# Another order for the last pairs of a windowed attention: blocks turned and low parts subtracted on other engines

## The chip, the cores and the metric

The kernel runs on one core of one Trainium2 chip, as one program. The metric is the device time of one execution, in microseconds (us). The core has five engines that each work through their own queue in order: PE (matrix products), DVE and ACT (elementwise work), POOL (elementwise work) and SP, which issues the transfers between the chip's main memory and the on-chip memory (SBUF). Products land in PSUM, a small memory of banks. Engines wait for each other by semaphores only.

## What is computed

Attention with a window and a few global keys, and behind it a "soft" mixture of experts on its output. The attention has 4 batches, 8 heads, 768 positions and a head size of 64:

```python
scores = scale * np.matmul(q, k.transpose(0, 1, 3, 2))
is_global = pos[None, :] < int(n_global)               # 8
is_local = (rel >= 0) & (rel < int(n_local))           # 96
bias = -slopes[:, None, None] * dist[None, :, :]
scores = np.where(is_global | is_local, scores + bias, -1000000000.0)
a = softmax(scores)                                     # over the keys
x = np.matmul(a, v)                                     # as 3072 tokens x 512
logits = x @ phi                                        # 32 slots, 4 of each of 8 experts
d, c = softmax(logits, over tokens), softmax(logits, over slots)
slot_out[e] = np.maximum((d.T @ x)[e] @ w1[e], 0) @ w2[e]
y = c @ slot_out
```

## The kernel before

**Pairs.** The attention goes through 16 pairs of heads, numbered 0 to 15 (four pairs of each batch; pairs 11 and 15 end the third and the fourth batch). Each pair is worked through in steps, and a step is one small function with one or a few instructions of one engine. The last number in a step's name is the head of the pair (0 or 1), or a part of a tile.

- `load_qk`, `load_v` (SP): the pair's inputs. `raw` tiles hold queries and keys, in turn for even and odd pairs.
- `scores u k` (PE, k = 0, 1, 2): products of keys and queries for a third of the blocks, into one of two PSUM tiles `sc`, in turn.
- `biased u k` (DVE): adds the table of distances, writes to a tile `tb` (three of them, in turn), and keeps a running maximum. The same `sc` tile is free for the next scores after it.
- `max_t` (PE) and `max_r` (DVE): the maximum over the partitions.
- `exponential u i` (ACT): in place on `tb`, for head i.
- `w_hi u i` (ACT): the weights rounded to 16 bits, into `ph`. `w_lo u i part` (POOL) or `w_lo_dve` (DVE): what the rounding lost, for a third of the blocks; three parts make the low half.
- `v_hi` (POOL), `v_hi_act` (ACT) or `v_hi_dve` (DVE), and `v_lo` (DVE): the same split for the values.
- `values u i` (PE): 39 products of the halves, into a bank `x`. It needs all three low parts; the next `w_hi` of the same head overwrites what it reads.
- `ev_sums`, `ev_recs`, `ev_mul u i` (DVE): the division, into token rows `xn`. They free the bank `x`.
- `tr u k` (PE): turns blocks of `xn`. `tr_copy u k` (ACT) or `tr_copy_dve u k` (DVE) copies the turned block out of PSUM into a tile `xt` (there are three, in `xta`, `xtt` and `tt`).
- `logits u` (PE) for odd pairs, then `logits_half` (ACT) or `logits_all` (DVE); and at the end of each batch `strip_max` (DVE), `strip_exp` (ACT), `by_token` (PE), `by_token_copy` and `lnat_copy` (ACT), `dispatch` (PE) and `dispatch_sum` (DVE), which bring the slots' inputs up to date.

**PSUM banks.** `max_t`, `tr`, `logits`, `by_token` and `dispatch` share two banks "m" in turn. Each of these steps can start only when the result of the step two before it (among these) has been read out.

**Order.** There is no scheduler: the list `ORDER` (line 55) has 607 steps, and each engine gets its instructions in the order in which the steps stand there. Two steps of one engine never pass each other.

**Weights.** Some 32 MB of expert weights stream in all the while. Ten tiles are theirs from the start. The steps `free n` (SP) load more of them into tiles of the attention, each when its last reader is done; the order of the last `free` of each tile also decides which piece of the weights it holds.

**Behind the list** come the last softmax over the slots, the hidden layer, the output products and the output's transfers (`last_dispatch` and the list `TAIL`). Three filler products (line 556) of `warm_x` stand at the very front of it.

Of the kernel before, what the change touches and what calls it, by code (L numbers as in the profile page):

```python
# [28 lines left out]
QW = KB + WIN  # L29
# [278 lines left out]
def tile_attention_moe(ctx: ExitStack, tc: tile.TileContext, qk, v, phi, w1, w2, nn, out):  # L308
    nc = tc.nc
# [58 lines left out]
    phi_ = [t[:, 0:PH].bitcast(F16) for t in pht]  # L368
# [84 lines left out]
    def blocks(w):  # L453
        return w[:, 0:6 * PB].rearrange("p (s c) -> p s c", c=PB)
# [44 lines left out]
    def tb(u):  # L499
        return tbuf[u % 3]  # L500
# [99 lines left out]

    def w_hi_dve(u, i):
        nc.vector.tensor_copy(out=blocks(phi_[i])[:, :, 0:QW], in_=tb(u)[:, i].rearrange("p (s c) -> p s c", c=QW))

    def w_lo(u, i, part, engine=None):
        c = slice(2 * part, 2 * part + 2)
        (engine or nc.gpsimd).tensor_tensor(out=blocks(plo_[i])[:, c, 0:QW], in0=tb(u)[:, i].rearrange("p (s c) -> p s c", c=QW)[:, c],  # L606
                                            in1=blocks(phi_[i])[:, c, 0:QW], op=ALU.subtract)

    def w_lo_dve(u, i, part):
        w_lo(u, i, part, nc.vector)  # L610

    def values(u, i):
        ph, pl = phi_[i], plo_[i]
        vh, vl = vhi[u % 2], vlo[u % 2]
        x = sums(u, i)
        ops = []
        for t in range(NJ):
            for j, c in ((t, PCOL[t]), (t - 1, PCOL[t - 1] + KB)):
                if j >= 0:
                    for w, vv, d in ((ph, vh, D + 1), (ph, vl, D), (pl, vh, D + 1)):  # L620
                        ops.append((t, c, w, vv, j, d))
        for z, (t, c, w, vv, j, d) in enumerate(ops):
            nc.tensor.matmul(out=x[:, (D + 1) * t:(D + 1) * t + d], lhsT=w[:, c:c + P], rhs=vv[:, j, i, 0:d],  # L623
                             start=(z == 0), stop=(z == len(ops) - 1), skip_group_check=True)
# [253 lines left out]

    def table_rest_act(u):
        table.rest(nc.scalar.copy)  # L880

    def table_pair_act(p):
        table.pair_act(p)

    def table_pair(p):
        table.pair(p)

    steps = dict(piece=piece_of, free=free, extra=extra, load_phis=load_phis, bcast=bcast, keys=keys, table_rest=table_rest, table_rest_act=table_rest_act, table_pair_act=table_pair_act, warm_x=warm_x, warm=warm,
                 table_even=table_even, table_odd=table_odd, table_pair=table_pair, load_qk=load_qk, load_v=load_v, v_hi=v_hi, v_hi_act=v_hi_act, v_hi_dve=v_hi_dve, v_lo=v_lo,
                 scores=scores, biased=biased, max_t=max_t, max_r=max_r, exponential=exponential, w_hi=w_hi, w_lo=w_lo, w_lo_dve=w_lo_dve, w_hi_dve=w_hi_dve,  # L890
                 values=values, ev_sum=ev_sum, ev_rec=ev_rec, ev_sums=ev_sums, ev_recs=ev_recs, ev_mul=ev_mul, tr=tr, tr_copy=tr_copy, tr_copy_dve=tr_copy_dve,
                 logits=logits, logits2=logits2, logits_half=logits_half, logits_all=logits_all, strip_max=strip_max, strip_exp=strip_exp,
                 strip_sum=strip_sum, by_token=by_token, by_token_copy=by_token_copy, lnat_copy=lnat_copy, dispatch=dispatch, dispatch_sum=dispatch_sum)
    late_constants()
    for name, u, *args in ORDER:
        steps[name](u, *args)
    left = LeftBanks()
    put_rest = last_dispatch(left, lambda: warm_x(last))
    att.close()


    tail = ExitStack()
# [327 lines left out]
```

## Time and profile before

| | us |
|---|---|
| median of 3 runs | 185.19 (184.1 to 185.4) |
| the profiled execution, its own time | 184.54 |
| its span, first to last instruction | 182.5 |
| PE at work | 170.5 (93% of the span) |
| DVE at work | 141.6 (78%) |
| ACT at work | 125.8 (69%) |
| POOL at work | 97.2 (53%) |

The span is what the trace covers; times in the trace count from its start. In the trace one instruction, or a few alike, is one row. An engine's "idle before" is the time that it stood before an instruction, with the work that ended the wait. The end of a product on PE is modelled, so a row may reach a little into the next one. All engines but SP are busy for most of the first 120 us, which are the attention; after that mainly PE and the transfers are.

### The profile page before, as it was taken

What the parts mean: (1) busy time and instruction counts of PE and PEld (TensorE: products, weight loads), DVE (VectorE), ACT (ScalarE), POOL (GpSimd) and SP (SyncE); (2) the same over time, 40 slices, a digit from 0 to 9 for tenths busy, and PEclk for the clock granted to TensorE, in tenths of its full rate; (3) what the DMA queues carried; (4) which work ended last, traced back from release to release, by engine and by line L of the source; (5) the groups of instructions that cost most, each with busy time, mean ns of one, the idle gap of its engine ahead of it and who ended that gap; (6) DMA issues with size and microseconds to landing.
All of it is one profiled execution on the core that took longest, in us unless ns stands there. A gap on an engine that the chain in (4) does not pass through costs nothing.

```text
span 182.5 us, 6745 instructions
## 1 busy us (share of the span) xinstructions
PE 170.5 (93%) x2805; PEld 125.8 (69%) x2805; DVE 141.6 (78%) x378; ACT 125.8 (69%) x164; POOL 97.2 (53%) x129
## 2 busy tenths in 40 slices
PE   8999899999999999999999998999899999999820
PEld 2567689797878877979888986875533256677710
DVE  5999999999998989899999999987867303346430
ACT  3499989999989999988999999953302120345320
POOL 6926689859799498797998996750010000000000
PEclk9999999999999999999999999999999999999975
DMA  6999999958998956789887399999999999989892
GB/s 186 420 399 390 413 400 392 392 192 307 381 391 338 383 156 247 250 310 379 288 344 276 89 310 376 407 370 416 416 387 409 408 404 404 380 303 405 347 334 65
DMA packets 15306, 61.41 MB, mean 337 GB/s; under 512 B 1698, under 2 KB 2850, under 8 KB 13474
## 3 DMA queue, kind: packets, MB, share of 16 engines
q1 hardware_dynamic: 15264, 60.89, 87.8%
q8 instruction: 24, 0.39, 0.9%
q14 instruction: 16, 0.13, 0.2%
q10 hardware_dynamic: 2, 0.00, 0.0%
HBM read 54.59 MB, written 6.29 MB: 334 GB/s over the span
## 4 chain that ended last, share of the span: by engine, by line


## 5 line engine op out<-in xcount | busy, mean ns | idle before, releaser
L606 POOL TENSOR_TENSOR ph<-tb,ph 128x432 f16<-128x432 f32 x83 | 85.9, 1066 | 18.9 <-ACT ph L599 15.8
L596 ACT ACTIVATE tb<-tb,nb 128x1296 f32<-128x1296 f32 x32 | 43.7, 1374 | 0.9 <-DVE nb L592 0.8
L623 PEld LDWEIGHTS <-ph 128*128 128x128 f16 x1248 | 40.7, 97 | 4.2 <-issue 2.8
L599 ACT CAST ph<-tb 128x1296 f16<-128x1296 f32 x32 | 40.6, 1271 | 2.8 <-PE x L623 0.9
L623 PE MATMUL x<-v,ph 128*128 128x65 f16 (+1 forms) x1209 | 42.0, 193 | 0.3 <-POOL ph L606 0.2
L571 PE MATMUL sc<-raw 64*128 64x216 f32 (+1 forms) x392 | 40.8, 340 | 0.0
L571 PEld LDWEIGHTS sc<-raw 64*128 64x128 f32 x392 | 32.3, 186 | 6.0 <-issue 3.5
L651 DVE CUSTOM_DVE_ANT_1 xn<-x,rc 120x448 f32<-120x448 f32 x31 | 18.3, 622 | 2.1 <-PE m L774 1.6
L580 DVE CUSTOM_DVE_ANT_1 tb<-sc,tt,mx 128x864 f32<-128x864 f32 x16 | 17.8, 1115 | 1.1 <-DVE mx L580 0.5
L549 DVE SCALAR_TENSOR_TENSOR v<-vt,v 128x896 f16<-128x896 f32 x14 | 16.2, 1159 | 0.0
L663 PE MATMUL m<-ident,xn 120*128 120x120 f32 x98 | 14.7, 276 | 0.2 <-DVE xmax L651 0.2
L663 PEld LDWEIGHTS m<-ident,xn 120*128 120x128 f32 x98 | 10.0, 141 | 2.7 <-issue 1.5
L104 PE MATMUL hp<-wp,sl 128*32 128x512 f32 x80 | 10.9, 594 | 0.3 <-ACT sl L99 0.3
L606 DVE TENSOR_TENSOR ph<-tb,ph 128x432 f16<-128x432 f32 x13 | 9.6, 765 | 0.0
L580 DVE CUSTOM_DVE_ANT_1 tb<-sc,xtt,mx 128x864 f32<-128x864 f32 x8 | 8.9, 1115 | 0.4 <-DVE mx L580 0.2
L580 DVE CUSTOM_DVE_ANT_1 tb<-sc,xta,mx 128x864 f32<-128x864 f32 x8 | 8.9, 1112 | 0.2
L542 ACT ACTIVATE v<-vt 128x896 f16<-128x896 f32 x9 | 8.6, 951 | 0.0
L205 PE MATMUL cp<-sos,ct 32*128 32x128 f32 (+1 forms) x120 | 8.4, 334 | 0.2 <-ACT ph L218 0.2
L159 PE MATMUL o<-wp,ht 128*32 128x128 f32 x256 | 8.4, 275 | 0.0
L580 DVE CUSTOM_DVE_ANT_1 tb<-sc,tt 128x864 f32<-128x864 f32 x8 | 8.4, 1050 | 0.0
L159 PEld LDWEIGHTS o<-wp,ht 128*32 128x32 f32 x256 | 6.6, 109 | 1.5 <-issue 1.0
L910 POOL MEMSET ht<- 128x536 f32 x1 | 0.5, 544 | 13.1 <-PE ld L848 13.1
(235 smaller groups left out, 283.5 us busy)
## 6 DMA issues: line engine op xcount, KB each, us to landing
raw<-in_qk_dram SPq DMA_DIRECT2D x14, 832.0 KB, 5.7
wp<-in_w_dram SPq DMA_DIRECT2D x10, 1024.0 KB, 8.0
wp<-in_w_dram SPq DMA_DIRECT2D x15, 512.0 KB, 9.0
vt<-in_v_dram SPq DMA_DIRECT2D x14, 448.0 KB, 5.5
tb<-in_w_dram SPq DMA_DIRECT2D x3, 1024.0 KB, 8.1
wp<-in_qk_dram SPq DMA_DIRECT2D x2, 832.0 KB, 9.5
raw<-in_w_dram SPq DMA_DIRECT2D x2, 832.0 KB, 4.5
ph<-in_w_dram SPq DMA_DIRECT2D x2, 768.0 KB, 9.9
```

Of the source, the lines that this page charges most:

```text
L104: self.nc.tensor.matmul(out=hp[n][32 * s:32 * s + 32, :], lhsT=slv(a, c, s), rhs=w1(4 * a + s, c // 2)[:, (c % 2) * DF + 512 * n:(c % 2) * ...
L159: nc.tensor.matmul(out=o[32 * s:32 * s + 32, o0:o0 + w], lhsT=ht[:, k:k + 32], rhs=w2(4 * a + s, half)[:, at:at + w], start=(a == 0 and c ...
L542: nc.scalar.activation(out=vhi[u % 2][:, :, :, 0:D], in_=vraws(u), func=AF.Copy, scale=V_SC)
L549: nc.vector.scalar_tensor_tensor(out=vlo[k].rearrange("p j i d -> p (j i) d"), in0=vraws(u).rearrange("p j i d -> p (j i) d"), scalar=V_SC ...
L571: nc.tensor.matmul(out=z[:, i, at:at + n], lhsT=r_[r, KCOL[j]:KCOL[j] + KR], rhs=r_[r, KW + KB * j:KW + KB * j + n], start=True, stop=True)
L580: nc.vector.tensor_tensor_reduce(out=tb(u)[:, :, BW * k:BW * k + BW], in0=sc[(3 * u + k) % 2][:, :, 0:BW], in1=table.unit(u % NP, k), scal ...
L596: nc.scalar.activation(out=t, in_=t, func=AF.Exp, bias=nbs[u], scale=T_SC)
L599: nc.scalar.copy(out=blocks(phi_[i])[:, :, 0:QW], in_=tb(u)[:, i].rearrange("p (s c) -> p s c", c=QW))
L606: (engine or nc.gpsimd).tensor_tensor(out=blocks(plo_[i])[:, c, 0:QW], in0=tb(u)[:, i].rearrange("p (s c) -> p s c", c=QW)[:, c], in1=bloc ...
L623: nc.tensor.matmul(out=x[:, (D + 1) * t:(D + 1) * t + d], lhsT=w[:, c:c + P], rhs=vv[:, j, i, 0:d], start=(z == 0), stop=(z == len(ops) - ...
L651: nc.vector.tensor_tensor_reduce(out=xnb[(u // 2) % 3][:, :, c:c + D], in0=by_query(u, i)[:, :, 0:D], in1=rcs.pop((u, i)).unsqueeze(2).to_ ...
L663: nc.tensor.transpose(out=m[:, at:at + KB], in_=xnb[(u // 2) % 3][:, t, P * (p % 2):P * (p % 2) + P], identity=ident[0:KB, 0:KB])
```

## The change

Up to `w_hi 11 0` (the high part of pair 11, the 420th step) the list stays as it is. The 187 steps behind it are put in another order. The set of steps is the same but for 16 that are traded between engines:

- turned blocks: 9 1, 11 0 and 12 1 are now copied by DVE, and 9 0, 13 1 and 12 0 by ACT (each was on the other of the two); 11 1 and 15 0 stay on DVE;
- low parts: (13, 0, 0), (14, 0, 0), (15, 1, 0) and (15, 1, 2) go from POOL to DVE, and (12, 0, 2), (14, 0, 2), (15, 0, 1) and (15, 0, 2) from DVE to POOL;
- the values' high half: pair 14 goes from ACT to POOL, pair 15 from POOL to DVE.

The `free` steps are regrouped as well. Before, the last six were v16 and ph0 pieces, `tb0`, and the three `xt` tiles; now `tb0` comes last of all. The diff, cut to its core (the list is one line; of its 187 moved steps the first few are shown):

```diff
@@ -52,7 +52,7 @@
-ORDER = [
...
-('exponential', 11, 0), ('w_hi', 11, 0), ('w_lo', 11, 0, 0), ('max_t', 12), ('max_r', 12), ('dispatch', 7), ('scores', 13, 1), ('w_lo', 11, 0, 1), ('biased', 13, 0),
...
+('exponential', 11, 0), ('w_hi', 11, 0), ('w_lo', 11, 0, 1), ('dispatch', 7), ('biased', 13, 0), ('w_lo', 11, 0, 0), ('ev_recs', 10), ('v_hi_act', 12), ('ev_mul', 10, 0),
...
@@ -597,6 +597,16 @@
+    def w_hi_part(u, i, part, copy=nc.scalar.copy):
+        c = slice(2 * part, 2 * part + 2)
+        copy(out=blocks(phi_[i])[:, c, 0:QW], in_=tb(u)[:, i].rearrange("p (s c) -> p s c", c=QW)[:, c])
+
+    def w_hi_part_dve(u, i, part):
+        w_hi_part(u, i, part, nc.vector.tensor_copy)
+
+    def w_hi_part_pool(u, i, part):
+        w_hi_part(u, i, part, nc.gpsimd.tensor_copy)
```

The new functions are entered in the table of steps, but no step of the list uses them. Lines behind 600 have a number that is higher by 10 in the changed kernel.

The first of three places is DVE's queue from the second `biased` of pair 15 to its third (the two rows each of L580; the maximum of the third is what `max_t 15` turns). Before:

```order
L580 ISA tb_95,mx<-sc_171,xtt,mx 128x2x432
L580 ISA mx 128x1
L672 COPY tt<-m 128x288
L549 SCALAR_TENSOR_TENSOR v_100<-vt,v_100 128x896
L580 ISA tb_95,mx<-sc_172,xtt,mx 128x2x432
```

And in the changed kernel:

```order
L580 ISA tb_95,mx<-sc_171,xtt,mx 128x2x432
L580 ISA mx 128x1
L754 COPY state<-al 128x1
L616 TENSOR_TENSOR ph_98<-tb_96,ph_98 128x2x216
L682 COPY tt<-m 128x480
L549 SCALAR_TENSOR_TENSOR v_100<-vt,v_100 128x896
L682 COPY tt<-m 128x288
L580 ISA tb_95,mx<-sc_172,xtt,mx 128x2x432
```

Between the two stand now, beside `v_lo 14` (L549) and one copy, also `strip_sum 3` (L754), the low part (13, 0, 0) (L616) and a second copy of a turned block of pair 11.

The second place is DVE's queue around `logits_all 11` (L710 before, L720 after) and `strip_max 11` (L727, L737), from the last division of pair 13 (L651, L661) on. Before:

```order
L651 ISA xn_106,xmax<-x,rc 120x7x64
L651 ISA xmax 120x1
L744 COPY state<-al 128x1
L710 ISA lsb,al<-m,lsb 96x240
L710 ISA al 96x1
L710 ISA lsb,al<-m,lsb 32x48
L710 ISA al 32x1
L727 TENSOR_SCALAR state<-al,state 128x1
L672 COPY xtt<-m 128x288
L606 TENSOR_TENSOR ph_98<-tb_97,ph_98 128x2x216 x2
L549 SCALAR_TENSOR_TENSOR v_100<-vt,v_100 128x896
```

And in the changed kernel:

```order
L661 ISA xn_106,xmax<-x,rc 120x7x64
L661 ISA xmax 120x1
L616 TENSOR_TENSOR ph_98<-tb_97,ph_98 128x2x216
L720 ISA lsb,al<-m,lsb 96x240
L720 ISA al 96x1
L720 ISA lsb,al<-m,lsb 32x48
L720 ISA al 32x1
L737 TENSOR_SCALAR state<-al,state 128x1
L616 TENSOR_TENSOR ph_98<-tb_97,ph_98 128x2x216
L545 TENSOR_SCALAR v_100<-vt 128x14x64
L682 COPY xta<-m 128x288
L549 SCALAR_TENSOR_TENSOR v_100<-vt,v_100 128x896
```

One of the two low parts of pair 14 (L606, L616) has moved ahead of `logits_all 11`, and `v_hi_dve 15` (L545) now stands ahead of `v_lo 15` (the last row of each).

The third place is the end of POOL's queue, from the low parts of (13, 0) on; `ph_99` is head 1 and `ph_98` head 0; `tb_96`, `tb_97` and `tb_95` here are pairs 13, 14 and 15. Before:

```order
L606 TENSOR_TENSOR ph_98<-tb_96,ph_98 128x2x216 x3
L539 TENSOR_SCALAR v_100<-vt 128x14x64
L606 TENSOR_TENSOR ph_99<-tb_97,ph_99 128x2x216 x3
L606 TENSOR_TENSOR ph_98<-tb_97,ph_98 128x2x216
L606 TENSOR_TENSOR ph_99<-tb_95,ph_99 128x2x216 x3
```

And in the changed kernel:

```order
L539 TENSOR_SCALAR v_100<-vt 128x14x64
L616 TENSOR_TENSOR ph_98<-tb_96,ph_98 128x2x216 x2
L616 TENSOR_TENSOR ph_99<-tb_97,ph_99 128x2x216 x3
L616 TENSOR_TENSOR ph_98<-tb_97,ph_98 128x2x216
L616 TENSOR_TENSOR ph_99<-tb_95,ph_99 128x2x216
L616 TENSOR_TENSOR ph_98<-tb_95,ph_98 128x2x216 x2
```

Before, POOL ended with the three low parts of (15, 1), and DVE did those of (15, 0). Now POOL does one of (15, 1) and two of (15, 0), and DVE the rest.

## Rows read from the trace of the kernel before

**Rows 1.** The page's slices: TensorE's granted clock in 40 equal slices of the span.

```profile
PEclk9999999999999999999999999999999999999975
```

**Rows 2.** Windows: stretch, its length; PE, PEld, DVE, ACT, POOL busy; clock; DMA.

```profile
90.40:112.30 21.90, 21.36 (x391) 18.39 (x387) 21.26 (x52) 21.44 (x24) 19.00 (x19) 1.00 0.78 271
112.30:127.00 14.70, 14.30 (x266) 10.70 (x267) 12.62 (x39) 10.48 (x19) 7.46 (x7) 1.00 1.01 396
...
133.90:175.00 41.10, 39.92 (x675) 22.95 (x674) 18.84 (x48) 11.53 (x30) 0.54 (x1) 1.00 0.97 379
```

**Rows 3.** Timeline of PE: start, length, line, operation, tiles, count [idle before <- releaser].

```profile
96.80 0.65 PE L623 MATMUL x<-v,ph 128*128 128x65 f16 x16 [0.17 <-POOL ph L606]
...
112.36 0.32 PE L587 MATMUL m<-ident,mx 128*128 128x128 f32 x1 [0.37 <-ACT xtt L668]
...
114.24 1.65 PE L623 MATMUL x<-v,ph 128*128 128x65 f16 x39
...
116.51 1.34 PE L623 MATMUL x<-v,ph 128*128 128x65 f16 x39
...
120.55 1.48 PE L623 MATMUL sc<-v,ph 128*128 128x65 f16 x39
...
123.17 0.91 PE L663 MATMUL sc<-ident,xn 120*128 120x120 f32 x7
...
126.91 0.72 PE L556 MATMUL x<-ident 128*128 128x256 bf16 x6
```

**Rows 4.** Timeline of DVE, 102 to 122 us (the fourth row from a narrower stretch).

```profile
102.91 1.89 DVE L549 SCALAR_TENSOR_TENSOR v<-vt,v 128x896 f16<-128x896 f32 x1
...
110.92 1.11 DVE L580 CUSTOM_DVE_ANT_1 tb<-sc,xtt,mx 128x864 f32<-128x864 f32 x1
...
114.04 0.40 DVE L710 CUSTOM_DVE_ANT_0 lsb<-m,lsb 96x240 f32<-96x240 f32 x1
...
115.34 1.26 DVE L606 TENSOR_TENSOR ph<-tb,ph 128x432 f16<-128x432 f32 x1
...
120.87 1.64 DVE L606 TENSOR_TENSOR ph<-tb,ph 128x432 f16<-128x432 f32 x3
```

**Rows 5.** Timeline of POOL, narrow stretches: two low parts in a row; one alone.

```profile
102.74 2.92 POOL L606 TENSOR_TENSOR ph<-tb,ph 128x432 f16<-128x432 f32 x2 [0.23 <-ACT ph L599]
...
117.33 1.67 POOL L606 TENSOR_TENSOR ph<-tb,ph 128x432 f16<-128x432 f32 x1 [1.18 <-ACT ph L599]
```

**Rows 6.** Timeline of ACT: the high parts of pair 15.

```profile
115.98 1.27 ACT L599 CAST ph<-tb 128x1296 f16<-128x1296 f32 x1 [0.23 <-PE x L623]
...
119.45 1.27 ACT L599 CAST ph<-tb 128x1296 f16<-128x1296 f32 x1
```

**Rows 7.** Lines 606 and 549: count; ns shortest/median/longest, first and last start.

```profile
L606 POOL TENSOR_TENSOR ph<-tb,ph x83: 999/1010/1859, 14.9 to 119.9; 128x432 f16<-128x432 f32 x83
...
L606 DVE TENSOR_TENSOR ph<-tb,ph x13: 595/605/1323, 16.5 to 121.9; 128x432 f16<-128x432 f32 x13
...
L549 DVE SCALAR_TENSOR_TENSOR v<-vt,v x14: 1077/1085/1892, 11.9 to 117.1; 128x896 f16<-128x896 f32 x14
```

**Rows 8.** DVE: one- and two-operand pass (timeline), and copies (groups; mean ns).

```profile
1.68 0.25 DVE L258 TENSOR_SCALAR xn<-xn 128x216 f32<-128x216 f32 x1
1.97 0.39 DVE L259 SCALAR_TENSOR_TENSOR xn<-xn 128x216 f32<-128x216 f32 x1
...
L672 DVE COPY xtt<-m 128x288 f32<-128x288 f32 x3 | 1.4, 457 | 0.1
L672 DVE COPY xta<-m 128x480 f32<-128x480 f32 x2 | 1.2, 623 | 0.0
```

**Rows 9.** SP's timeline, the page's transfers (KB, us to landing), PE's timeline.

```profile
122.62 0.50 SPq L413 DMA_DIRECT2D tb<-in_w_dram  x1
...
tb<-in_w_dram SPq DMA_DIRECT2D x3, 1024.0 KB, 8.1
...
147.50 0.38 PE L159 MATMUL x<-tb,ht 128*32 128x256 f32 x1
```

More of the change, by code (lines that the diff above doesn't have):

```diff
@@ L889, in tile_attention_moe @@
                  table_even=table_even, table_odd=table_odd, table_pair=table_pair, load_qk=load_qk, load_v=load_v, v_hi=v_hi, v_hi_act=v_hi_act, v_hi_dve=v_hi_dve, v_lo=v_lo,
-                 scores=scores, biased=biased, max_t=max_t, max_r=max_r, exponential=exponential, w_hi=w_hi, w_lo=w_lo, w_lo_dve=w_lo_dve, w_hi_dve=w_hi_dve,
+                 scores=scores, biased=biased, max_t=max_t, max_r=max_r, exponential=exponential, w_hi=w_hi, w_lo=w_lo, w_lo_dve=w_lo_dve, w_hi_dve=w_hi_dve, w_hi_part=w_hi_part, w_hi_part_dve=w_hi_part_dve, w_hi_part_pool=w_hi_part_pool,
                  values=values, ev_sum=ev_sum, ev_rec=ev_rec, ev_sums=ev_sums, ev_recs=ev_recs, ev_mul=ev_mul, tr=tr, tr_copy=tr_copy, tr_copy_dve=tr_copy_dve,
```

2 lines of the change are left out of this document (1 added, 1 removed).

## Prediction

> **What bounds the kernel now.** I read the windows first, then each engine's timeline from 82 to 130 us, then the tail. From 90.4 to 127 us, the stretch that the change rewrites, PE is at work for 21.36 of 21.90 us and 14.30 of 14.70 us, at a granted clock of 1.00 [rows 1, 2]: it lacks work for only 0.54 + 0.40 = 0.94 us. Some more is hidden in stretched passes: one pass of values (39 products) lasts 1.34 us when nothing is missing, but 1.65 at 114.24 and 1.48 at 120.55 [rows 3]: 0.31 + 0.14. Passes like these, before 97 and at 122, add about 0.3 more. So PE waits for some 1.7 us in all. That is the most a new order can win, since the set of PE instructions stays the same.
>
> The other engines are hardly freer: up to 112.3 DVE works 21.26 and ACT 21.44 of 21.90 us, POOL 19.00 [rows 2]. Behind 126.91, where PE's three filler products begin [rows 3], everything is as before: a chain of last softmax, hidden layers and output that keeps PE at work for 39.92 of the 41.10 us to 175 [rows 2]. So the end moves with the last PE step of the attention, us for us. The reader is to see here that the question is only: does the last pass of values, which ended with the transposes' start at 123.17 [rows 3], end earlier or later?
>
> **A second resource.** The low parts (w_lo on POOL, w_lo_dve on DVE) and v_lo on DVE each read two SBUF operands, and these never overlap in time. Alone they take 1.01, 0.60 and 1.08 us (the medians), at most 1.86, 1.32 and 1.89 [rows 7]. The longest are the meetings: POOL's part at 102.74 ends at 103.85; v_lo, issued at 102.91, ends at 104.80, which is 0.95 behind it; POOL's next part then ends at 105.66 [rows 4, 5]. So whichever starts first runs, and the other waits for its end. From such pairs: v_lo ends 0.95 us after the POOL part that it met, w_lo_dve 0.46 after (115.34 + 1.26 = 116.60, behind a POOL part from 115.13), a POOL part 0.87 after DVE's (117.33 + 1.67 = 119.00) [rows 4, 5]. I call it the shared door.
>
> **The change, part by part.** I walk the new order from the first moved step with the old durations; a time with no row is worked out so.
>
> *Traded steps.* The counts of parts are equal: POOL has four new low parts for four, DVE four for four. ACT loses v_hi_act 14 and gets short copies, so it is relieved by about 0.7 us. DVE gets v_hi_dve 15, which this trace never shows. Lower bound: in one early pair DVE's one-operand pass over 216 columns took 0.25 us and a two-operand pass 0.39 [rows 8]; 896 columns at the same saving of 0.14 per 216 give 1.08 - 0.58 = 0.50. Upper bound: v_lo's own 1.08 over these 896 elements. I take 0.60, nearest the early row, which is of the same instruction. The Trainium skill, VectorE: DVE Perf Modes, section "The perf-mode tier table (the rule you actually need)", says that tensor_scalar on fp32 in SBUF runs at twice the rate of tensor_tensor. The rule's estimate is (896 / 2 + 150) / 0.96 GHz = 0.62 us, the sum it would give is the same to 0.02 us, and no run here shows this shape. At 1.08 the forecast would lose 0.3 us more, since v_lo 15 and two low parts stand behind it.
>
> *Up to 97.3 us: nothing.* dispatch 7 and max_t 12 change places. The pass of pair 11's first head still waits for its last low part on POOL [rows 3] and ends at 97.3 as before.
>
> *97.3 to 105: +0.3.* The new PE order runs without a wait through the scores of 14 and the first scores of 15. But the part (12, 0, 2) now goes to POOL, so POOL does all six of pair 12 in a row from 97.70: 98.57, 99.54, 100.51, 101.48, 102.45, and v_lo 13 gets the door before the sixth, which ends at 104.27. The pass of (12, 0), ready on PE at 103.5, has to wait there and ends at 105.2. Before, the same PE steps were done by 104.9.
>
> *105 to 114: +0.4, in place of the +0.3.* DVE now does, between the second and the third biased of pair 15: strip_sum 0.15; w_lo_dve (13, 0, 0), which meets POOL's (13, 0, 2), 1.07; tr_copy_dve 11 0, 0.57; v_lo 14, which meets POOL's (13, 0, 1), 1.25; tr_copy_dve 11 1, 0.37 (copies issue some 0.08 apart from the durations in [rows 8]). The third biased begins at 111.6, against 110.92 [rows 4]. max_t 15 waits for it, and runs at 112.8 instead of 112.36 [rows 3]. Behind max_t 15 on PE stand logits 11 and everything else.
>
> *114 to 119: +1.1.* w_lo_dve (14, 0, 0) now stands ahead of logits_all 11. It is issued at 114.43; POOL starts (14, 0, 2) at 114.32, so DVE waits until 115.33 and ends at 115.79. logits_all 11 begins at 115.7 instead of 114.04 [rows 4]. Two engines wait for it. PE: tr 12 1 needs the bank that logits 11 filled, so PE stands 0.8 us, then 0.4 more for by_token 11, which needs strip_exp 11. ACT: strip_exp 11 stands ahead of w_hi 15 1, so w_hi 15 1 begins at 117.3 instead of 115.98 [rows 6]. The pass of (14, 0) ends at 118.8, where it was 117.7 (116.51 and 39 products [rows 3]).
>
> *119 to 124.7: +1.5.* w_hi 15 0 begins at 120.5 instead of 119.45 [rows 6]. Before, its three low parts ran on DVE in one row of 1.64 us [rows 4]. Now one is on DVE and two are on POOL, through one door: POOL 121.8 to 122.8, DVE to 123.3, POOL to 124.2. The last pass waits for that, with 16 products still to do, and ends at 124.7, against 123.17 [rows 3].
>
> *Behind that: 0.* dispatch_sum 11 moves ahead of the last division, on time that DVE has; the last transposes, copies and logits are as they were.
>
> *Transfers: 0.* The frees on SP are regrouped: tb0 (1 MB) goes last, behind the last logits, some 6 us later than 122.62; with the 8.1 us of such transfers it lands by 138. The first product with a second-layer weight in tb is at 147.50 [rows 9]. The holders only swap pieces among second-layer weights. The cover is about 9 us; if it were gone, each us late would be a us at the end.
>
> The sum: 184.54 (the profiled execution, span 182.5 and 2.0 around it) + 1.5 = 186.0. The median of the runs shown, 185.19, lies 0.65 above that execution, so the same sum from there is 186.7. I put the forecast between, 186.3.
>
> **The rivals.**
>
> *The door falls the other way.* At 114.4 the two passes are issued 0.1 us apart, less than my walk can tell. If DVE goes first, logits_all 11 starts at 115.0, PE does not stand for it, and only the low parts of pair 15 remain: +0.8, so 185.3 to 186.0. It speaks against it that three delays of DVE come before.
>
> *Slower by over 1% (187.04; about what a measurement of this kernel can tell from no change).* One queue decides: on ACT strip_exp 11 stands ahead of w_hi 15 1, and waits for DVE. My walk has it start at 116.7, with ACT idle for 1.0 us. From there on each us by which DVE is later is a us for all that ACT has left and for the last pass. If logits_all 11 ends 0.5 us or more later than 116.4 (one more meeting, 0.46 to 0.95 [rows 4, 5]), the end is at +2.0 to +2.5: 187.2. For it: DVE has no slack up to there [rows 2]. Against it: none of the walk's other waits is so near a tie.
>
> *The waits even out, or fall.* PE's present waits (0.37 at 112.36 for a copy on ACT, the stretched pass at 114.24 [rows 3]) go away, since ACT is relieved, and mine do not come: 184.54 - 1.7 = 182.8 at the best, 184 more likely. Against it: DVE and POOL get no less to do.
>
> *The clock.* PE's waits today are at most 0.37 us with the clock at 1.00 [rows 1, 3]; two of 0.7 and 0.8 are longer than any that these rows cover. If the clock fell to 1.2 GHz behind one, each us of products would cost up to one more, 2 us or more in all: over 188. The Trainium skill, TensorE: Matmul & The Clock Gate, section "What's actually happening", says that the array's clock is halved after it has been idle; these rows show only that 0.37 us does not do it.
>
> **How the numbers follow.** The walk as it stands 0.42; the door the other way 0.18; the late queue 0.25; waits even out or fall 0.12, of which a third by over 1%; the clock 0.03. Slower by over 1%: 0.25 + 0.03 = 0.28. Faster by over 1%: 0.04. Within 1%: 0.68. The range leaves out the best of the one end and the clock at the other: 184.3 to 187.8.
>
> **What would show it.** In the changed profile: v_lo 13 and v_lo 14 longer than 1.08; the third biased of pair 15 past 111; logits_all 11 past 115.5 with PE's wait before tr 12 1 named after DVE lsb; w_hi 15 1 past 117; the last low parts alternating POOL, DVE, POOL; the filler products at 128.4 instead of 126.91; and from there the same 55.6 us to the end. The prediction is wrong if PE has no wait over 0.5 us between 110 and 120, if logits_all 11 starts by 114.5, or if the stretch behind the filler changes its length.

## The result, and the profile after

The changed kernel takes 186.44 us (median, 186.28 to 186.71) where the kernel before, run beside it, takes 184.98 (184.1 to 185.4). The ratio is 1.0091, its 95% interval 1.0066 to 1.0116: slower by some 1.5 us, and within the 1% to which the prediction gave .68, though the interval reaches a little past it. The profiled execution took 186.32, its span is 184.2.

The page of the changed kernel, its span, busy time by engine, and TensorE's granted clock in 40 slices:

```profile
span 184.2 us, 6745 instructions
...
PE 171.4 (93%) x2805; PEld 125.9 (68%) x2805; DVE 143.6 (78%) x379; ACT 125.6 (68%) x163; POOL 98.0 (53%) x129
...
PEclk9999999999999999999999999999999999999995
```

Nothing here tells slower from equal: the shares are those of before. The windows do (columns as in [rows 2]). This trace begins 0.30 us earlier than the other against its work (w_hi 11 0, the last step ahead of the part of the list that was changed, starts at 92.04 instead of 91.73), so its stretches are set 0.30 later:

```profile
90.70:112.60 21.90, 21.71 (x391) 18.39 (x387) 21.47 (x51) 20.57 (x21) 20.44 (x19) 1.00 0.85 304
112.60:128.84 16.24, 14.47 (x266) 10.56 (x265) 14.32 (x41) 11.07 (x19) 6.82 (x7) 1.00 0.92 336
135.80:176.90 41.10, 39.98 (x675) 23.02 (x674) 18.77 (x48) 11.48 (x30) 0.55 (x1) 1.00 0.95 370
```

In the first 21.90 us PE gets through 391 rows, as before, though it is at work for 0.35 us longer (21.71 instead of 21.36). The next 266 take it 16.24 us up to the filler products; before they took 14.61 (112.30 to 126.91 [rows 2, 3]). So all of the 1.63 us is lost on PE behind 112.6; what causes it may lie earlier on the other engines. The 41.10 us behind the filler hold the same 675 rows and the same busy time as before. From here on I measure each kernel by its **stretch**, from the start of w_hi 11 0 to the start of the filler: 126.91 - 91.73 = 35.17 before (from unrounded times), 36.81 after. From the filler to the last product it is 47.72 and 47.74 us. ACT's rows of w_hi 11 0, before and after:

```profile
91.73 1.27 ACT L599 CAST ph<-tb 128x1296 f16<-128x1296 f32 x1
...
92.04 1.27 ACT L599 CAST ph<-tb 128x1296 f16<-128x1296 f32 x1
```

A stretch is read from one trace each. How far it can be trusted shows in the changed kernel and the four kernels below whose lists are the same up to max_t 15 and whose first change comes behind it: there max_t 15 comes 21.20 to 21.22 us behind w_hi 11 0.

PE's timeline in the changed kernel, the rows that answer [rows 3] and the waits between them:

```profile
104.05 1.65 PE L633 MATMUL x<-v,ph 128*128 128x65 f16 x39
...
113.24 0.29 PE L587 MATMUL m<-ident,mx 128*128 128x128 f32 x1 [0.60 <-DVE rsall L649]
...
114.93 0.53 PE L673 MATMUL m<-ident,xn 120*128 120x120 f32 x3 [0.46 <-DVE xmax L661]
115.29 1.35 PE L633 MATMUL x<-v,ph 128*128 128x65 f16 x39
116.88 0.50 PE L673 MATMUL m<-ident,xn 120*128 120x120 f32 x3 [0.24 <-DVE al L720]
117.66 0.43 PE L761 MATMUL m<-ident,ex 128*120 128x128 f32 x2 [0.28 <-ACT ex L744]
...
123.36 1.88 PE L633 MATMUL x<-v,ph 128*128 128x65 f16 x39
125.08 0.91 PE L673 MATMUL sc<-ident,xn 120*128 120x120 f32 x7
...
128.84 0.72 PE L556 MATMUL x<-ident 128*128 128x256 bf16 x6
```

Four waits of 0.24 to 0.60 us now name DVE, or ACT, which waits for DVE, and the last pass of values is 1.88 us long where one that misses nothing takes 1.35. The two waits of before are gone (max_t 15 for a copy on ACT, the stretched pass at 114.24).

DVE's timeline around the places of [rows 4], with the pass v_hi_dve 15 (line 545):

```profile
102.16 1.60 DVE L549 SCALAR_TENSOR_TENSOR v<-vt,v 128x896 f16<-128x896 f32 x1
...
108.55 1.32 DVE L616 TENSOR_TENSOR ph<-tb,ph 128x432 f16<-128x432 f32 x1
...
110.36 1.33 DVE L549 SCALAR_TENSOR_TENSOR v<-vt,v 128x896 f16<-128x896 f32 x1
...
111.98 1.10 DVE L580 CUSTOM_DVE_ANT_1 tb<-sc,xtt,mx 128x864 f32<-128x864 f32 x1
...
114.79 1.39 DVE L616 TENSOR_TENSOR ph<-tb,ph 128x432 f16<-128x432 f32 x1
116.10 0.39 DVE L720 CUSTOM_DVE_ANT_0 lsb<-m,lsb 96x240 f32<-96x240 f32 x1
...
117.42 0.62 DVE L545 TENSOR_SCALAR v<-vt 128x896 f16<-128x896 f32 x1
```

POOL's timeline, narrow stretches (a low part of pair 12, the low part (14, 0, 2), the last one (15, 0, 2)):

```profile
102.77 1.85 POOL L616 TENSOR_TENSOR ph<-tb,ph 128x432 f16<-128x432 f32 x1
...
114.69 1.02 POOL L616 TENSOR_TENSOR ph<-tb,ph 128x432 f16<-128x432 f32 x1
...
123.16 1.37 POOL L616 TENSOR_TENSOR ph<-tb,ph 128x432 f16<-128x432 f32 x1
```

The waits at the shared door lie inside these lengths. The pass at 114.79 on DVE, alone 0.60, is issued 0.10 behind POOL's of 114.69, which ends at 115.71; it ends at 116.18, 0.47 behind that. logits_all 11 (line 720) stands right behind it. So the engines do not wait for each other by semaphores only: no idle time is shown before this pass, and its wait lies inside its own length.

ACT's timeline: strip_exp 11, and the high parts of pair 15, which answer [rows 6]:

```profile
117.02 0.49 ACT L744 ACTIVATE ex<-lsb,state 128x240 f32<-128x240 f32 x1 [0.94 <-DVE state L737]
...
117.70 1.25 ACT L599 CAST ph<-tb 128x1296 f16<-128x1296 f32 x1
...
120.84 1.27 ACT L599 CAST ph<-tb 128x1296 f16<-128x1296 f32 x1
```

SP's timeline and the transfers issued from 129 to 142 us (KB, us to landing):

```profile
129.67 0.46 SPq L413 DMA_DIRECT2D tb<-in_w_dram  x1
...
tb<-in_w_dram SPq DMA_DIRECT2D x1, 1024.0 KB, 10.5
```

### The profile page after: what moved, and what is told of

The parts are those of the page before. It is cut to its first block, busy times and chain, and to the rows that moved or that the text cites. A ratio compares the mean times of both kernels' runs of the same rounds, so it can differ in the third digit from the quotient of the medians.

```text
span 184.2 us, 6745 instructions
## 1 busy us (share of the span) xinstructions
PE 171.4 (93%) x2805; PEld 125.9 (68%) x2805; DVE 143.6 (78%) x379; ACT 125.6 (68%) x163; POOL 98.0 (53%) x129
## 4 chain that ended last, share of the span: by engine, by line
## 5 line engine op out<-in xcount | busy, mean ns | idle before, releaser
L616 POOL TENSOR_TENSOR ph<-tb,ph 128x432 f16<-128x432 f32 x83 | 86.7, 1075 | 23.5 <-ACT ph L599 22.3
L633 PE MATMUL x<-v,ph 128*128 128x65 f16 (+1 forms) x1209 | 42.6, 193 | 0.4
L661 DVE CUSTOM_DVE_ANT_1 xn<-x,rc 120x448 f32<-120x448 f32 x31 | 18.3, 622 | 1.4 <-PE m L784 0.9
L580 DVE CUSTOM_DVE_ANT_1 tb<-sc,tt,mx 128x864 f32<-128x864 f32 x16 | 17.8, 1114 | 1.1 <-DVE mx L580 0.7
L549 DVE SCALAR_TENSOR_TENSOR v<-vt,v 128x896 f16<-128x896 f32 x14 | 16.2, 1156 | 0.0
L616 DVE TENSOR_TENSOR ph<-tb,ph 128x432 f16<-128x432 f32 x13 | 11.5, 895 | 0.0
L580 DVE CUSTOM_DVE_ANT_1 tb<-sc,xtt,mx 128x864 f32<-128x864 f32 x8 | 8.9, 1114 | 0.4 <-DVE mx L580 0.2
L580 DVE CUSTOM_DVE_ANT_1 tb<-sc,xta,mx 128x864 f32<-128x864 f32 x8 | 8.9, 1111 | 0.0
L580 DVE CUSTOM_DVE_ANT_1 tb<-sc,tt 128x864 f32<-128x864 f32 x8 | 8.4, 1051 | 0.2 <-PE sc L571 0.2
L542 ACT ACTIVATE v<-vt 128x896 f16<-128x896 f32 x8 | 7.6, 953 | 0.0
L104 PEld LDWEIGHTS hp<-wp,sl 128*32 128x32 f32 x80 | 2.8, 110 | 6.4 <-issue 6.0
```

The source lines that it names most:

```text
L104: self.nc.tensor.matmul(out=hp[n][32 * s:32 * s + 32, :], lhsT=slv(a, c, s), rhs=w1(4 * a + s, c // 2)[:, (c % 2) * DF + 512 * n:(c % 2) * ...
L549: nc.vector.scalar_tensor_tensor(out=vlo[k].rearrange("p j i d -> p (j i) d"), in0=vraws(u).rearrange("p j i d -> p (j i) d"), scalar=V_SC ...
L580: nc.vector.tensor_tensor_reduce(out=tb(u)[:, :, BW * k:BW * k + BW], in0=sc[(3 * u + k) % 2][:, :, 0:BW], in1=table.unit(u % NP, k), scal ...
L661: nc.vector.tensor_tensor_reduce(out=xnb[(u // 2) % 3][:, :, c:c + D], in0=by_query(u, i)[:, :, 0:D], in1=rcs.pop((u, i)).unsqueeze(2).to_ ...
```

## The experiments

All twelve, each against the kernel before on the same chip. "Stretch" is taken from each kernel's own trace. The intervals of most of these kernels overlap one another, so what tells them apart below is the stretch and the rows; for the pass twice the six runs lie between 186.90 and 189.63 us, and its time is unclear.

| kernel | median us | ratio [95%] | stretch |
|---|---|---|---|
| changed | 186.44 | 1.0091 [1.0066, 1.0116] | 36.81 |
| new list to step 479, then old | 184.85 | 1.0007 [0.9992, 1.0021] | 35.51 |
| new list to step 515, then old | 185.10 | 1.0014 [0.9999, 1.0028] | 35.64 |
| old list to step 514, then new | 185.37 | 1.0031 [1.0016, 1.0045] | 36.15 |
| the pass behind strip_max 11 | 185.35 | 1.0033 [1.0019, 1.0047] | 35.88 |
| the pass twice | 188.14 | 1.0197 [1.0147, 1.0247] | 37.47 |
| the pass without the door | 185.71 | 1.0045 [1.0023, 1.0067] | 36.03 |
| copy 11 0 on ACT | 185.77 | 1.0062 [1.0037, 1.0088] | 36.33 |
| the same, v_lo 14 without the door | 185.42 | 1.0024 [1.0005, 1.0042] | 35.95 |
| (12, 0, 2) on DVE again | 185.33 | 1.0028 [1.0002, 1.0053] | 35.77 |
| last low part on DVE | 186.69 | 1.0112 [1.0089, 1.0134] | 36.83 |
| three undone at once | 186.16 | 1.0079 [1.0055, 1.0103] | 36.31 |
| old list, v_hi 15 later | 185.31 | 1.0022 [1.0003, 1.0040] | 35.59 |

**Which part of the list costs it.** Three kernels follow one order up to a step and then do what is left in the other's. The seam of the first:

```diff
 ('tr_copy_dve', 11, 1), ('w_lo', 13, 0, 1),
-('tr', 10, 0), ('tr_copy', 10, 0), ('biased', 15, 2),
+('free', 1), ('values', 13, 0), ('v_hi', 15), ('w_lo', 14, 1, 0),
```

> The first half of the new order (up to the third biased of pair 15, where both orders have done all but two of the same steps), then the old order. Theory of the walk: the two halves lose about 0.4 and 1.1 us, one behind the other. The first half's loss is DVE's stack ahead of the third biased of pair 15; so here max_t 15 comes some 0.4 to 0.7 us late, logits_all 11 by as much, and the end at +0.4 to +0.7 us, a ratio of 1.002 to 1.004 to the kernel before. Rival 1, all of it is lost in the first half: 1.009. Rival 2, all of it is lost in the second half: 1.000.

The second, the old order up to step 514 and the new behind:

```diff
 ('values', 13, 1), ('w_lo', 13, 0, 1),
-('free', 1), ('values', 13, 0), ('v_hi', 15),
+('strip_sum', 3), ('w_hi', 14, 1), ('tr', 10, 0),
```

> The old order up to the same point, then the second half of the new order. Theory of the walk: logits_all 11 stands behind a low part of pair 14 that meets POOL's at the shared door, and pair 15's last low parts alternate between POOL and DVE; the end at +0.7 to +1.1 us, a ratio of 1.004 to 1.006. The stretch from w_hi 11 0 to the filler products, 35.18 us before and 36.80 changed, should be 35.9 to 36.3. Rival 1, all lost in the first half: 1.000, 35.2. Rival 2, all lost in the second half: 1.009, 36.8.

The third, the new order for its first 59 moved steps only:

```diff
 ('biased', 14, 2), ('values', 12, 0),
-('biased', 15, 0), ('max_t', 14), ('w_lo', 13, 1, 1),
+('tr_copy_dve', 9, 0), ('w_lo', 13, 1, 0), ('w_lo', 13, 1, 1),
```

> The new order only as far as the first scores of pair 15, then the old one. Theory of the walk: the pass of (12, 0) waits for its sixth part on POOL and ends 0.3 us late, but DVE has a pass less to do up to here, and this, not PE's 0.3, decides what comes behind: the end between 0 and +0.3 us, a ratio of 1.000 to 1.002. Rival: PE's 0.3 us stays and is the first part of the loss, and the copies left over add to it: 1.003 or more.

In the stretch the halves cost 0.47 and 0.98, which makes 1.45 of 1.64; by the ratios 0.0014 and 0.0031 of 0.0091, both below what was expected. So the halves do not quite add; that the first half's delay is dearer with the second behind it is one reading, which these three kernels alone don't show. In the first half max_t 15 came as late as in the changed kernel (21.22 us behind w_hi 11 0), as expected. With the first third alone, the 0.33 us in the stretch are not shown to be the late pass of (12, 0): max_t 15 stood 0.69 us there for a copy on ACT.

In the second half the size came as expected (36.15), but not the way to it. In that kernel w_lo_dve (14, 0, 0) was issued 0.05 us ahead of POOL's next part, lasted 0.61, and POOL had to wait. That is the rival "the door the other way", not the meeting that was expected, and the pass of (14, 1) then waited for POOL. PE in that kernel:

```profile
114.44 0.50 PE L633 MATMUL x<-v,ph 128*128 128x65 f16 x11
115.80 1.02 PE L633 MATMUL x<-v,ph 128*128 128x65 f16 x28 [0.86 <-POOL ph L616]
```

**The pass ahead of logits_all 11.** First it is moved behind the step for which two engines wait:

```diff
-('w_lo_dve', 14, 0, 0), ('free', 16),
+('free', 16),
...
-('logits_all', 11), ('strip_max', 11),
+('logits_all', 11), ('strip_max', 11), ('w_lo_dve', 14, 0, 0),
```

> The changed kernel with one step moved: the low part (14, 0, 0) on DVE goes behind logits_all 11 and strip_max 11, as it stood before the change. Theory (the queue before strip_max): logits_all 11 begins at about 114.8 instead of 116.1, PE's waits ahead of tr 12 1 and by_token 11 go, w_hi 15 1 begins near 116.7 instead of 117.7, and the end is 0.9 us earlier than in the changed kernel, 0.6 to 1.1 of the 1.5 lost: a ratio of 1.003 to 1.006 to the kernel before. Rival (DVE's total is what counts, and it is unchanged): no gain, 1.009.

The stretch fell by 0.93, to 35.88. logits_all 11 began at 114.52, w_hi 15 1 at 116.46 (114.81 and 116.75 against the changed kernel's trace, which starts 0.29 earlier), and PE had no wait at tr 12 1. The expectation takes this for the old place of the part, but before the change POOL did it: the move makes a third order, not the old one. DVE's row of logits_all 11:

```profile
114.52 0.40 DVE L720 CUSTOM_DVE_ANT_0 lsb<-m,lsb 96x240 f32<-96x240 f32 x1
```

Then the opposite, the same pass twice:

```diff
-('logits_all', 11), ('strip_max', 11),
+('w_lo_dve', 14, 0, 0), ('logits_all', 11), ('strip_max', 11),
```

> The changed kernel with DVE's low part (14, 0, 0) done twice in a row, with the same result: 0.5 us more on DVE ahead of logits_all 11, at a moment when POOL has nothing to do. Theory (from there each us on DVE is a us at the end): logits_all 11, strip_exp 11, w_hi 15 1 and the end are 0.5 us later: stretch 37.3, ratio 1.011 to 1.012. Rival (there is slack behind it, as ACT and PE have idle time): 36.8 to 36.9, 1.009.

The stretch grew by 0.66, and logits_all 11 by the same (24.72 us behind w_hi 11 0, not 24.06). So a delay there is passed on whole. The time grew by more, 1.7 us between the medians, with runs far apart; the profiled execution shows 0.83 of it behind the filler, where it takes 56.14 us to the end and the changed kernel 55.31. The products there end as always (47.74 behind the filler), so it is in the last output writes; why is not settled.

What this run shows besides is the clock. PE's longest wait of all runs, and the window around it:

```profile
118.04 0.44 PE L761 MATMUL m<-ident,ex 128*120 128x128 f32 x2 [1.31 <-ACT ex L744]
...
115.60:119.00 3.40, 2.09 (x49) 1.85 (x46) 3.29 (x11) 1.82 (x5) 0.00 (x0) 1.00 0.78 302
```

PE stood for 1.31 us at once and the granted clock was 1.00 throughout, the higher level.

Is it the pass's work or its wait? The third kernel leaves the pass where it is, at the same size, but takes one operand from PSUM:

```diff
-('w_lo_dve', 14, 0, 0),
+('w_lo_psum', 14, 0, 0),
...
+    def w_lo_psum(u, i, part):
+        c = slice(2 * part, 2 * part + 2)
+        nc.vector.scalar_tensor_tensor(out=blocks(plo_[i])[:, c, 0:QW], in0=sc[0][:, :, 0:QW], scalar=0.0,
+                                       in1=tb(u)[:, i].rearrange("p (s c) -> p s c", c=QW)[:, c], op0=ALU.mult, op1=ALU.mult)
```

> The changed kernel, but DVE's pass for the low part (14, 0, 0) now reads one operand from PSUM and only one from SBUF, at the same size and the same place in the queue (it writes zeros: the low part (14, 0, 0) is left out of the result). Theory (the shared door): the pass no longer waits for POOL's (14, 0, 2), so it lasts 0.6 to 0.7 us instead of 1.39; logits_all 11 begins 0.7 to 0.8 earlier than in the changed kernel, and the stretch from w_hi 11 0 to the filler products falls from 36.81 to 36.0 to 36.2, ratio to before 1.004 to 1.006. POOL's (14, 0, 2) stays near 1.0. Rival (DVE is late by its amount of work, or the pass waits for something else that it reads): the pass still ends after 116, stretch 36.6 to 36.9, ratio 1.008 to 1.010.

DVE and POOL in that kernel:

```profile
114.52 0.60 DVE L621 SCALAR_TENSOR_TENSOR ph<-sc,tb 128x432 f16<-128x432 f32 x1
115.04 0.39 DVE L730 CUSTOM_DVE_ANT_0 lsb<-m,lsb 96x240 f32<-96x240 f32 x1
...
114.42 1.01 POOL L616 TENSOR_TENSOR ph<-tb,ph 128x432 f16<-128x432 f32 x1
```

DVE's pass runs from 114.52 to 115.12 inside POOL's, from 114.42 to 115.43, and neither is longer than alone. Where passes with two SBUF operands each meet in the rows above, one is longer by its wait. logits_all 11 came 0.78 earlier and the stretch was 0.78 shorter: the door alone is worth 0.78 of the 1.64, at this one place.

**What makes the third biased of pair 15 late.** The prediction added it up from DVE's work ahead of it, copies and meetings alike, so a copy is taken away:

```diff
-('tr_copy_dve', 11, 0),
+('tr_copy', 11, 0),
```

> The changed kernel with one trade undone: the turned block 11 0 is copied by ACT again, so DVE's stack ahead of the third biased of pair 15 is 0.57 us shorter and ACT does 0.46 us more. Theory (DVE's stack ahead of the third biased sets max_t 15): max_t 15 comes 0.4 to 0.6 us earlier, PE's wait of 0.60 before it nearly goes, and as DVE then meets POOL's next part instead, the end is 0.4 to 0.5 us earlier: stretch 36.3 to 36.4, ratio 1.006 to 1.007. Rival (the meeting at the low part (14, 0, 0) sets the end, whenever max_t 15 comes): no gain, 36.8, 1.009.

The size came true, 0.48 less, and the place did not, so the size is luck. The third biased stayed 19.97 us behind w_hi 11 0 (19.94 in the changed kernel). DVE and POOL:

```profile
109.53 1.90 DVE L549 SCALAR_TENSOR_TENSOR v<-vt,v 128x896 f16<-128x896 f32 x1
...
111.72 1.10 DVE L580 CUSTOM_DVE_ANT_1 tb<-sc,xtt,mx 128x864 f32<-128x864 f32 x1
...
114.52 0.87 DVE L616 TENSOR_TENSOR ph<-tb,ph 128x432 f16<-128x432 f32 x1
...
109.09 1.38 POOL L616 TENSOR_TENSOR ph<-tb,ph 128x432 f16<-128x432 f32 x1
...
114.89 1.38 POOL L616 TENSOR_TENSOR ph<-tb,ph 128x432 f16<-128x432 f32 x1
```

v_lo 14 was issued 0.54 earlier (17.78 us behind w_hi 11 0, not 18.32) and became 0.57 longer (1.33 to 1.90): it waits for POOL's (13, 0, 1), which ends at 110.47, and ends 0.96 behind it. The gain came from the next meeting: w_lo_dve (14, 0, 0) lasted 0.87. DVE did not come to it any earlier (22.78 us behind w_hi 11 0, 22.75 in the changed kernel). POOL came later: the copy on ACT put w_hi 14 1 back by 0.47, and with it POOL's row for pair 14, so that (14, 0, 2) started at 23.14 instead of 22.66, and DVE went ahead of it. So the gain was owed to the work that ACT got, not to the work that DVE lost. Next the same kernel with v_lo 14 off the door:

```diff
-('tr_copy_dve', 11, 0),
+('tr_copy', 11, 0),
...
-('v_lo', 14),
+('v_lo_psum', 14),
...
+    def v_lo_psum(u):
+        k = u % 2
+        rows = lambda x: x.rearrange("p j i d -> p (j i) d")
+        nc.vector.scalar_tensor_tensor(out=rows(vlo[k]), in0=sc[0][:, 0:1, 0:D].to_broadcast([P, 14, D]), scalar=0.0, in1=rows(vraws(u)), op0=ALU.mult, op1=ALU.mult)
```

> The kernel of the copy experiment (tr_copy 11 0 on ACT), and v_lo 14 reads one operand from PSUM and one from SBUF (it writes zeros: the low half of pair 14's values is left out of the result). Theory: v_lo 14 does not wait for POOL's (13, 0, 1), so it lasts 1.1 to 1.2 us instead of 1.90, the third biased of pair 15 begins 19.2 to 19.4 after w_hi 11 0 instead of 19.97, and max_t 15 and logits 11 come 0.4 to 0.7 earlier; the stretch falls from 36.33 to 35.7 to 36.0, if w_lo_dve (14, 0, 0) does not meet POOL for longer than it did there (0.87). Rival 1 (the third biased waits for something else): it stays at 19.9 to 20.0. Rival 2 (the gain is given back at the next meeting on the door, as in the kernel with three parts undone): third biased earlier, but w_lo_dve (14, 0, 0) over 1.0 us and a stretch of 36.2 to 36.5.

```profile
109.61 1.08 DVE L627 SCALAR_TENSOR_TENSOR v<-sc,vt 128x896 f16<-128x896 f32 x1
...
110.97 1.10 DVE L580 CUSTOM_DVE_ANT_1 tb<-sc,xtt,mx 128x864 f32<-128x864 f32 x1
...
109.18 1.38 POOL L616 TENSOR_TENSOR ph<-tb,ph 128x432 f16<-128x432 f32 x1
```

In these rows (DVE, then POOL) v_lo lies beside POOL's part and has its 1.08 us; the third biased comes 19.13 behind w_hi 11 0, 0.84 earlier than with the door. So what holds the third biased here is POOL's part and the door, and, with the copy experiment, not the amount of DVE's work. Of the 0.84 only 0.38 reached the filler: DVE took the door next, and PE waited 0.69 for POOL's late part of (14, 1).

**The part that POOL took over early.** One low part of pair 12 goes back to DVE, some 60 steps ahead of all this:

```diff
-('w_lo', 12, 0, 2), ('ev_mul', 11, 0),
+('ev_mul', 11, 0),
...
-('v_lo', 13),
+('w_lo_dve', 12, 0, 2), ('v_lo', 13),
```

> The changed kernel, but the low part (12, 0, 2) is done by DVE again, just ahead of v_lo 13. Theory: POOL has five parts of pair 12 instead of six, so the pass (12, 0) does not wait (1.3 us instead of 1.65), but DVE has 0.6 us more ahead of the third biased of pair 15, which sets the end: stretch 37.0 to 37.3 against 36.81, ratio 1.010 to 1.013. Rival (POOL's parts set the third biased through v_lo 14, not DVE's amount of work): POOL is 0.6 to 1.0 earlier at (13, 0, 1), the third biased comes earlier, stretch 36.2 to 36.6, ratio 1.005 to 1.008.

The rival was right, and by more than it said: the stretch fell by 1.04 to 35.77, though POOL was only 0.36 earlier at (13, 0, 1), where the rival had 0.6 to 1.0. DVE twice, then POOL:

```profile
102.04 1.12 DVE L616 TENSOR_TENSOR ph<-tb,ph 128x432 f16<-128x432 f32 x1
103.08 1.08 DVE L549 SCALAR_TENSOR_TENSOR v<-vt,v 128x896 f16<-128x896 f32 x1
...
114.37 0.64 DVE L616 TENSOR_TENSOR ph<-tb,ph 128x432 f16<-128x432 f32 x1
114.94 0.39 DVE L720 CUSTOM_DVE_ANT_0 lsb<-m,lsb 96x240 f32<-96x240 f32 x1
...
114.51 1.37 POOL L616 TENSOR_TENSOR ph<-tb,ph 128x432 f16<-128x432 f32 x1
```

DVE has more work and is earlier. The pass (12, 0) is 1.35 instead of 1.65, v_lo 13 meets nobody, w_lo_dve (13, 0, 0) meets nobody (0.60 instead of 1.32), and the third biased comes 0.29 earlier. Those 0.29 us carry DVE to 114.37, ahead of POOL's part at 114.51, so DVE goes through first: 0.64 instead of 1.39. 0.29 + 0.75 = 1.04. POOL's part before that one was still under way until 114.55, and DVE's pass ended 0.46 behind it: DVE waited for the part under way and went ahead of the next.

**The last low parts.** (15, 0, 2) goes back to DVE:

```diff
-('w_lo_dve', 15, 0, 0),
+('w_lo_dve', 15, 0, 0), ('w_lo_dve', 15, 0, 2),
...
-('w_lo', 15, 0, 2),
```

> The changed kernel with one trade undone: the last low part (15, 0, 2) runs on DVE, behind (15, 0, 0), and not as the third in the row POOL, DVE, POOL. Theory (the row through the shared door ends last): the last part is ready at about 124.2 instead of 124.5, the last pass of values, which lasts 1.88 us in the changed kernel, lasts 1.5 to 1.6, and the end comes 0.3 us earlier: the stretch from w_hi 11 0 to the filler products, 36.81 us in the changed kernel, at 36.5, a ratio of 1.006 to 1.008 to the kernel before. Rival (DVE is behind, and one more pass on it delays the divisions behind it by as much): no gain, 36.8 or more, 1.009 or more.

The last pass was shorter, 1.66, and the transposes behind it came 0.20 earlier, but the filler did not (36.83), since DVE's last division came 0.49 later. That division, and PE's transposes of pair 15:

```profile
125.91 0.62 DVE L661 CUSTOM_DVE_ANT_1 xn<-x,rc 120x448 f32<-120x448 f32 x1
...
126.60 0.63 PE L673 MATMUL x<-ident,xn 120*128 120x120 f32 x4 [0.15 <-DVE xmax L661]
```

The low part costs DVE what it saves PE: the rival.

**Three undone at once.** The copy on ACT, the pass behind strip_max 11 and the last part on DVE:

```diff
-('tr_copy_dve', 11, 0),
+('tr_copy', 11, 0),
...
-('logits_all', 11), ('strip_max', 11),
+('logits_all', 11), ('strip_max', 11), ('w_lo_dve', 14, 0, 0),
...
-('w_lo_dve', 15, 0, 0),
+('w_lo_dve', 15, 0, 0), ('w_lo_dve', 15, 0, 2),
```

> The changed kernel with the three named causes undone at once: (14, 0, 0) behind strip_max 11, (15, 0, 2) on DVE, the copy of 11 0 on ACT. Theory: they lie one behind the other on the same path and add up, 0.93 (measured alone) + 0.3 + 0.4 to 0.5: stretch 35.0 to 35.3, which is the kernel before's 35.17, ratio 0.999 to 1.002. Rival (they share one cause, and undoing the largest is nearly all there is): 35.7 to 35.9, 1.003 to 1.004.

A miss for both sides: 36.31, worse than with one of the three alone (35.88). DVE came to its pass at 115.87, when POOL had (14, 0, 2) under way since 115.43 (late again by the copy on ACT): 1.04 us instead of 0.60. By that DVE came to v_lo 15 just behind POOL's next part (DVE, then POOL):

```profile
118.37 1.93 DVE L549 SCALAR_TENSOR_TENSOR v<-vt,v 128x896 f16<-128x896 f32 x1
...
118.35 1.01 POOL L616 TENSOR_TENSOR ph<-tb,ph 128x432 f16<-128x432 f32 x1 [1.91 <-ACT ph L599]
```

It was 0.02 us too late, and lasted 1.93 us instead of 1.08. ACT's w_hi 15 1 and w_hi 15 0 were as early as with the one step moved, but DVE's last division was 0.89 us later. The three do not add, since each shifts who meets whom.

**A try at a faster kernel.** In the kernel before, v_hi 15 stands ahead of POOL's parts of pair 14; here it stands behind the fourth:

```diff
-('v_hi', 15), ('w_lo', 14, 1, 0),
+('w_lo', 14, 1, 0),
...
-('w_lo', 14, 0, 0),
+('w_lo', 14, 0, 0), ('v_hi', 15),
```

> The kernel before, with one move: v_hi 15 on POOL goes behind the low part (14, 0, 0), so that POOL's parts of pair 14 start up to 1 us earlier. An attempt at a kernel that beats both. If the stretched pass of (14, 1) (1.65 us) is owed to POOL's late parts: stretch 34.8 to 35.0 against 35.17, ratio 0.997 to 0.999. Rival (v_lo 15 then waits for v_hi 15, or the parts meet DVE's instead): stretch 35.2 to 35.6, ratio 1.000 to 1.003.

The pass (14, 1) got its 0.30 us back (1.65 to 1.35), but PE lost more at the next, as the rival had it: the pass (14, 0) took 2.07. PE waited 0.56 there for DVE's low part (1.33 long, it met v_hi 15 on POOL). 35.59 is 0.42 over the kernel before. No kernel here beats that one; the nearest are those with the first third and with the first half alone, whose times can't be told from it.

## Why the prediction was right, and where not

The forecast was 186.3 (184.3 to 187.8), with .68 on "within 1%": 186.44 came. Of the likeliest case nearly every time came true, though not the places of PE's waits. Measured times are given here less the 0.30 by which this trace starts early:

| step | forecast | measured |
|---|---|---|
| third biased of pair 15 begins | 111.6 | 111.68 |
| max_t 15 | 112.8 | 112.94 |
| w_lo_dve (14, 0, 0) issued, ends | 114.43, 115.79 | 114.49, 115.88 |
| logits_all 11 | 115.7 | 115.80 |
| strip_exp 11, w_hi 15 1 | 116.7, 117.3 | 116.72, 117.40 |
| w_hi 15 0 | 120.5 | 120.54 |
| transposes behind the last pass | 124.7 | 124.78 |
| filler products | 128.4 | 128.54 |

- **The sum.** +1.5 forecast, +1.64 in the stretch, +1.46 between the medians, +1.78 between the profiled executions. That 186.3, placed halfway between the sums 186.0 and 186.7 for no stated reason, was hit to 0.14 is luck.
- **The bound.** Right for the products: behind the filler they kept their length (47.74 us), so their end moved with the last step of the attention. From the filler to the end of the span it was 55.31 us where the prediction had 55.6 (55.55 before). These 0.24 us lie behind the last product, and over the traces of all kernels that length goes from 55.25 to 56.14, so the end follows PE only to some tenths of a us.
- **The shared door.** Right, and now shown by taking an operand away, at two places: the overlap appears, and the wait goes. Its figures hold: DVE's low part ends 0.47 behind POOL's, v_lo 0.95 to 0.96, POOL's part 0.86 to 0.87 behind DVE's.
- **97.3 to 105, "+0.3".** The wait of the pass (12, 0) came (1.65 us). The step put it as swallowed by the next ("in place of the +0.3"). What causes it, POOL's sixth part of pair 12, is not swallowed: without it POOL ends (13, 0, 1) 0.30 us earlier, the third biased comes 0.29 earlier, and this decides at 114.4 who gets the door: 1.04 of 1.64.
- **105 to 114, "+0.4".** The time was right to 0.1, the way it was added up was not. The walk had both meetings, but counted the copies on top. DVE's stack had room for a copy of 0.57: v_lo 14 ended 0.95 to 0.96 behind POOL's part with the copy ahead of it and without. The term is POOL's lateness and the door.
- **114 to 119, "+1.1".** The mechanism was right: moving the pass away gives 0.93, taking its door away 0.78, doubling it costs 0.66. PE's waits were spread otherwise: 0.24 before tr 12 1 and 0.28 before by_token 11, not 0.8 and 0.4, since PE had stood 0.60 and 0.46 at max_t 15 and tr 13 1 already. So the sign "a wait over 0.5 us" came true, at another step than the one it was meant for.
- **119 to 124.7, the last low parts.** POOL, DVE, POOL as forecast, and the last pass waited (1.88). But this term was worth nothing at the end: with it undone, and the rest left as it is, DVE's division was the next to be late.
- **v_hi_dve 15.** 0.62 where 0.60 was taken, but it is not free of the door, see below. By the Trainium skill, VectorE: DVE Perf Modes, section "The perf-mode tier table (the rule you actually need)", the estimate was 0.62, and the trace agrees.
- **Transfers.** tb0 was issued 7 us later (129.67) and took 10.5 us. The 8.1 of the prediction is the median of three; this same transfer took 9.9 before (122.62 to 132.49). So it landed at 140.1 and not by 138. The first product with a second-layer weight in tb was at 151.19, so the cover held with 11 us.
- **The rivals.** The door the other way did not happen in the changed kernel; in the kernel with (12, 0, 2) on DVE it did, at +0.60 in the stretch where +0.8 was forecast. The tie was 0.10 us wide, as the prediction said; that it fell to the likeliest case is luck, since the walk could not tell so little. The waits did not even out, and no queue was later than the walk. The clock stayed at 1.00 through all of these waits, up to 1.31 us in the kernel with the doubled pass; and the prediction's "at most 0.37" for the waits of before missed one of 0.57 at 21.5 us. The Trainium skill, TensorE: Matmul & The Clock Gate, section "What's actually happening", has the clock fall after idle time. No wait of these kernels' attention was followed by a fall. In one kernel, the first half, it did fall under the last products: PE was at work for 1.71 of the 2.00 us from 172 to 174 at 1.00, with no wait there over 0.38, and from 175 to 176 the granted clock was 0.50, the lower of its two levels (1.2 GHz). Its last product ended 48.19 us behind the filler, not 47.7, which the stretch does not count.

What stays open: the writes at the end of the kernel with the doubled pass, the 0.60 us that remain of 1.64 when (12, 0, 2) is on DVE, and what the changed kernel would take with (12, 0, 2) on DVE and the pass behind strip_max 11 together. The two weren't run as one, and after the three undone at once I would not add their gains.

## What to carry to other kernels

Where two engines wait for each other at a shared resource, a new order is worth what its meetings are worth, as this case shows: walk both queues through each meeting, and mark those where the two arrive within some tenths of a us, for there a delay that looks absorbed becomes a whole operation's length. A copy taken off the engine that seems late did not move the step that it was meant to move; one part taken off the other engine, 70 steps earlier in the list, gave back 1.04 of 1.64. And the single repairs did not add up (0.93, 0.48 and nothing gave 0.50 together), so each has to be measured with the others in place.

## What the runs showed that I had not expected

A pass with one SBUF operand can meet the door as well. v_hi_dve 15 takes 0.62 us in the changed kernel, where POOL is idle beside it. In the kernel with v_lo 14 off the door POOL's low part was under way (DVE, then POOL):

```profile
115.84 1.43 DVE L545 TENSOR_SCALAR v<-vt 128x896 f16<-128x896 f32 x1
...
115.41 1.37 POOL L616 TENSOR_TENSOR ph<-tb,ph 128x432 f16<-128x432 f32 x1
```

POOL's part ends at 116.78 and DVE's pass at 117.27, 0.49 behind it; the second-half kernel shows the same 1.43 us, 0.48 behind POOL's end. On POOL too: in the old list with v_hi 15 later, a low part on DVE that met that one-operand pass took 1.33 us and ended 0.45 behind it. But the passes with one operand in SBUF and one in PSUM did not wait (0.60 and 1.08 us beside POOL's).

The Trainium skill, SBUF — State Buffer, section "Who interferes with whom", draws the line there: on DVE it is the passes with two SBUF inputs, and tensor_scalar and copies in a mode that uses both ports, which contend with POOL; one SBUF input outside such a mode does not. These rows agree with it. The prediction counted operands only, and so priced v_hi_dve 15 as if it could never wait; in the changed kernel that cost nothing, since POOL happened to be idle.
